# A planned attention, GLU and soft-MoE kernel: all short scores ahead of the pooling of v, the slots' input in two halves, two rules of the plan changed, and a new plan

## The chip, the cores and the metric

The kernel runs on one core of one Trainium2 chip. The metric is the device time of one execution in microseconds; of the kernel before, three runs are shown (median 522.01). A profile is one further execution, recorded by the hardware profiler. The core has a matrix engine (PE, with its weight loads PEld shown apart), three engines for elementwise work (DVE, ACT and POOL), a queue that issues all DMAs (SP), an on-chip memory for tiles, and eight banks of accumulation memory (`ps`), into which alone PE writes.

## The reference

```python
# attention: per (batch 4, head 8), 576 positions of 64
q_d, k_d, v_d = means over groups of 4 positions             # 144 positions: the "short" attention
out_up = repeat(softmax(q_d k_d^T / 8) v_d, 4)
out_local = softmax(q k^T / 8 where |i - j| < 4) v           # a band
x = (out_up + out_local)  as 2304 tokens x 512
# GLU: 512 -> 1536 -> 512
x = (x @ w_a * (x @ w_b)) @ w_out
# soft mixture of experts: 32 slots, 8 experts
logits = x @ phi
d = softmax(logits, over the tokens);  slot_input = d.T @ x  # 32 x 512
slot_out[e] = relu(slot_input[e] @ w1[e]) @ w2[e]            # 8 experts of 4 slots
out = softmax(logits, over the slots) @ slot_out
```

## The kernel before

The whole kernel is one program of small tasks. A task names its engine, an assumed duration, the tasks it depends on, a priority, and the buffers and banks that it takes and gives back. `Plan.run` plays the tasks through on assumed times and thereby fixes, once and for all, in which order each engine gets its instructions. `LOOK` says for each engine how much later than the earliest possible task another one may start and still win by priority; `WT` and `ALTW` say when a task may go to its second engine; `BATCH` says between which planned times, and how far, PE keeps the large products together instead of letting a small task in between; `PR_D`, `PR_P`, `SOON` and `CB` are priorities. On the chip each engine then takes its instructions strictly in that order and waits for what an instruction needs.

Where the plan sees PE idle early on, it puts in products without use (`warm`, L360, on the tile `acc`); they fill PE's queue up to about 42 us.

The work in the order of the tokens:

- **Short attention** (`plan_datt`), once per batch of 5 pairs. `plan_load` sums q and k over groups of four (L412 on DVE, or L415 and L417 on POOL) into `dT`. Then three groups n = 2, 0, 1 of `dscore` (L631), `dmax`, `dexp` (L662 on ACT), `drec`, `dnorm` (L320 on POOL, into `dk` and in place), `dptr` (transposes, L694, L698, L701), evictions into `dpt` and `dpr`, and `dout` (L735), which is evicted into `xd` (L750). In the first batch v is pooled by PE too: `dvmm` (L599, two tasks of 8 products each in the trace).
- **The band** (`plan_pair`), 20 pairs of 116 tokens: `score` (L449, L459), `smax` (L467), `ssub` (L473), `sexp` (L479), `ssum` (L483 to L487), `snorm` (L320), `ptr` (L497), `pev`, `pv` (L511), then the sum with `xd` (L520), split into a high and a low part, the tile `x`.
- **Weights** (`plan_piece`): 36 pieces of 512 KB arrive as 64-bit words in a ring of four staging buffers (SP, L861 and L863) and are rebuilt as floats by four instructions: `clow` (ACT, L834), `cabs` (ACT, L839), `cbits` (DVE, L843) and `csign` (DVE, L848), which gives the staging buffer back for the next load. Pieces 1 to 8 are the first third of w_a and w_b, 9 to 16 the second, 17 to 28 w_out transposed, 29 to 36 the last third. Pieces of w_a and w_b are then split into a high part (ACT) and a low part (POOL). Those of w_out are multiplied with phi (`omm`, L893, six tasks of two pieces) into `wpr` (L991, L996), so that the logits come from the GLU's product without w_out.
- **GLU** (`plan_unit`): 18 tiles x 3 thirds x 2 halves, 108 halves of 12 products each (L1023). Below, "0a" is a half with the first third of w_a, "2b" one with the last third of w_b, and a *run* is a number of halves that stand on PE with nothing between them. A half is followed by the product a*b (L1038), its transposes (L1045), an eviction (L315), and per two tiles by the logits (L1059) and a chain of softmax steps (`k1` to `k12`).
- **Tail** (`plan_tail`): the gathered sums are transposed (`atr`), the slots' input is 12 products 512 wide (`slot_in`, L1295), evicted (`si_ev`, L1302, ACT), transposed (`si_tr`, L1307), copied (`si_t`, L1313, DVE); then the experts' first layer (`l1`, L1328), the second (`l2`, L1417), and the output (L1464). Between these stand nine transposes of the gates (`ctr`, L1384), their high parts (`chi`, L1389, ACT) and their low parts (`clo`, L1396, DVE subtractions).

Of the kernel before, what the change touches and what calls it, by code (L numbers as in the profile page):

```python
# [22 lines left out]
NCH = NTILES // 2  # L23
# [252 lines left out]
def tile_attn_glu_softmoe(  # L276
# [30 lines left out]
    def psum(shape=(128, 512)):  # L307
        return pp.tile(list(shape), F32, tag="ps", name="ps")
# [261 lines left out]
    def plan_datt(b):  # L570
# [184 lines left out]
        vv = []  # L755
        for f in range(4):
            o = pr + 0.1 + 0.01 * f
            if b < WIDE:
                if f % 2:
                    continue  # L760
                tl = add("D", c_dma(524288), lambda f=f: dvload2(f // 2), prio=o - 2.0, acq=("g",), lat=2.0)
                tv = add("PE", 1.8, lambda f=f: dvmm(f), [tl], o, acq=("ps",), rel=("g",))
                vv.append(add(
                    "A", 0.37, lambda e, f=f: dvev(f, e), [tv, T.get(("dvp", b))], o, acq=() if f else ("dv",),
                    rel=("ps",), alt=("V", 0.4, WT["ev"]),
                ))
# [14 lines left out]
        for n in (2, 0, 1):  # L781
# [5 lines left out]
            tn.append(t1)  # L787
            t2 = add("V", 1.0 if n < 2 else 0.7, lambda n=n: dmax(n), [t1], o)
# [436 lines left out]
    def plan_tail():  # L1225
# [65 lines left out]
        def slot_in():  # L1291
            X["sps"] = ps = psum()
            for ft in range(12):
# [3 lines left out]
                    rhs=X.pop(("o", ft // 4, ft % 4)), start=(ft < 4), stop=(ft >= 8),  # L1297
                )

        def si_ev():  # L1300
            X["si"] = sb(mp, "a", (128, 512))
            nc.scalar.activation(out=X["si"], in_=X.pop("sps"), func=ACTF.Copy, scale=li)  # L1302

        def si_tr():
            X["stp"] = ps = psum((128, 4, 32))
            for dt in range(4):
# [8 lines left out]
        t = add("PE", 2.9, slot_in, ta + [t for n in range(3) for t in T["rows", n]], -2000, acq=("ps",))
        add("N", 0.0, lambda: [X.pop(("ot", n)) for n in range(3)], [t], 0, rel=("w8x",) * 3, lat=0.0)
        t = add("A", 0.58, si_ev, [t, t_sc], -50, acq=("a",), rel=("ps",))
        t = add("PE", 0.9, si_tr, [t], -2000, acq=("ps",), rel=("a",))
        t_si = add("V", 0.3, si_t, [t], -50, rel=("ps",))

        hs = []
        for eg in range(2):
            for hf in range(2):
# [50 lines left out]
        for i0 in range(0, NTILES, n):  # L1374
# [30 lines left out]
            tc_.append(add("V", 0.8, clo, [t], 50, rel=("ps",)))  # L1405
# [123 lines left out]
LOOK = dict(PE=0.07, V=0.23, A=0.03, G=0.79, D=0.1, N=0.0)  # L1529
WT = dict(pool=6.14, dvp=2.32, clo=4.65, clow=0.83, chi=7.15, norm=1.54, ev=0.86, xhi=7.17)  # L1530
# [12 lines left out]
CB = [-14.41, 0.63, -2.7, 0.8, 2.84, 13.81]  # L1543
# [50 lines left out]
```

## Time and profile before

| | us |
|---|---|
| median of 3 runs | 522.01 (521.02 to 522.11) |
| the profiled execution | 521.47 |
| its span in the trace | 519.7 |
| PE busy | 506.4 |
| DVE / ACT / POOL busy | 249.8 / 220.7 / 108.2 |

The span is what the trace covers; 1.77 us of the profiled execution lie around it. PE is busy nearly all the time, so the profile is to be read stage by stage: what PE's busy time consists of (early on, the products without use), where it waits, and what its tasks cost in the order in which they stand.

### The profile page before, as it was taken

Reading aid. Unit: us, or ns where it says so; the run is one execution under the profiler, and the core shown is the slowest. Engines: PE = TensorE matmul, PEld = TensorE weight load, DVE = VectorE, ACT = ScalarE, POOL = GpSimd, SP = SyncE. Lnnn points to the kernel's source line nnn. Section 1 sums busy time; section 2 is a strip of 40 time slices with the busy share of each in tenths; the row PEclk is TensorE's granted clock in tenths of the full one; section 3 lists DMA queues with packets and bytes.
Section 4 is the critical chain, followed back from the end, with each engine's and each line's share of the span. In section 5 each row is a group of like instructions: output and inputs, shape, how many; then the busy total and the mean of one; then the engine's idle time right before and its main releaser. Section 6 shows DMA issues by size and latency. Waiting matters only on the chain.

```text
span 519.7 us, 11193 instructions
## 1 busy us (share of the span) xinstructions
PE 506.4 (97%) x4605; PEld 387.7 (75%) x4605; DVE 249.8 (48%) x581; ACT 220.7 (42%) x533; POOL 108.2 (21%) x159
## 2 busy tenths in 40 slices
PE   8999998999999999999999999999999999989995
PEld 8888864677778777787777877878787778753484
DVE  5899888864387631453731341221234542245022
ACT  1888777864343432423532232222244532242132
POOL 0767657452133220330211000000000000020000
PEclk9999998999999999999999999999999999999997
DMA  8977688900152200321000000000076486999996
GB/s 318 389 224 259 215 262 283 325 34 0 42 180 90 77 2 1 108 81 55 26 2 0 21 21 2 21 1 1 1 279 205 145 343 255 370 399 420 420 356 252
DMA packets 23010, 84.25 MB, mean 162 GB/s; under 512 B 2992, under 2 KB 3888, under 8 KB 19376
## 3 DMA queue, kind: packets, MB, share of 16 engines
q1 hardware_dynamic: 22960, 83.54, 44.4%
q8 instruction: 36, 0.59, 0.5%
q14 instruction: 14, 0.11, 0.1%
HBM read 78.81 MB, written 4.72 MB: 161 GB/s over the span
## 4 chain that ended last, share of the span: by engine, by line
PE 87%; DMA 6%; DVE 2%; ACT 2%; issue 1%; POOL 1%; SPq 0%; ACTq 0%; DVEq 0%; POOLq 0%
PE ps L1023 55%; PE ps L1045 5%; PE ps L1059 3%; DMA w<-in_w_outt_dram 3%; DMA w<-in_moe_w_a_dram 3%; PE ps L1417 3%; PE ps L1328 3%; PE ps L511 3%; PE ps L360 2%; PE ps L1184 2%; PE ps L497 2%; PE ps L735 2%; PE ps L1464 1%; PE ps L459 1%; PE ps L631 1%; PE ps L694 1%
## 5 line engine op out<-in xcount | busy, mean ns | idle before, releaser
L1023 PE MATMUL ps<-w,x 128*128 128x512 f32 x1296 | 313.3, 396 | 0.4 <-ACT a L315 0.4
L1023 PEld LDWEIGHTS ps<-w,x 128*128 128x128 f32 x1296 | 239.3, 188 | 57.6 <-issue 5.4
L1038 DVE TENSOR_TENSOR g<-a,ps 128x512 f32<-128x512 f32 x51 | 34.8, 683 | 94.1 <-PE ps L1023 94.0
L315 ACT COPY a<-ps 128x512 f32<-128x512 f32 x51 | 29.8, 585 | 88.8 <-PE ps L1023 88.8
L315 ACT COPY gT<-ps 128x512 f32<-128x512 f32 x53 | 30.5, 586 | 49.3 <-PE ps L1045 49.2
L320 POOL TENSOR_TENSOR e<-e,mx 128x512 f32<-128x512 f32 x20 | 20.9, 1044 | 90.5 <-DVE mx L487 78.3
L320 POOL TENSOR_TENSOR w<-cv,w 128x512 fp32r<-128x512 f32 x24 | 31.1, 1303 | 23.8 <-ACT w L315 20.0
L1172 POOL TENSOR_TENSOR cn<-ce,cs 128x64 f32<-128x64 f32 x9 | 2.6, 293 | 145.3 <-DVE cs L1169 100.5
L1045 PE MATMUL ps<-cst,g 128*128 128x128 f32 x216 | 32.3, 277 | 0.0
L834 ACT ACTIVATE w<-w 128x512 uint32<-128x512 uint32 x36 | 24.5, 684 | 15.4 <-DMA w<-in_w_outt_dram 6.6
L1045 PEld LDWEIGHTS ps<-cst,g 128*128 128x128 f32 x216 | 24.9, 141 | 7.3 <-issue 1.6
L843 DVE SCALAR_TENSOR_TENSOR ps<-ps,w 128x512 uint32<-128x512 uint32 x36 | 24.9, 692 | 5.3 <-ACT ps L839 5.0
L848 DVE SCALAR_TENSOR_TENSOR cv<-w,ps 128x512 uint32<-128x512 uint32 x36 | 24.7, 687 | 2.8
L360 PE MATMUL ps<-acc 128*128 128x128 f32 x150 | 21.7, 297 | 1.2 <-POOL acc L355 1.2
L839 ACT ACTIVATE ps<-w 128x512 f32<-128x512 f32 x36 | 22.9, 640 | 0.0
L360 PEld LDWEIGHTS ps<-acc 128*128 128x128 f32 x150 | 19.9, 208 | 1.9 <-POOL acc L355 1.2
L320 DVE TENSOR_TENSOR x<-xn,x 128x256 fp32r<-128x256 f32 (+16 forms) x36 | 17.4, 512 | 4.8 <-ACT x L315 4.4
L412 DVE TENSOR_REDUCE dT<-qk 128x116 f32<-128x464 f32 (+1 forms) x28 | 16.3, 623 | 5.6 <-DMA qk<-in_qk_dram 5.6
L467 DVE TENSOR_REDUCE mx<-ps 128x4 f32<-128x256 f32 x40 | 15.0, 417 | 7.5 <-PE ps L459 7.4
L843 DVE SCALAR_TENSOR_TENSOR ps<-ps,w8x 128x512 uint32<-128x512 uint32 x12 | 8.4, 696 | 20.2 <-ACT ps L839 20.2
L520 DVE TENSOR_TENSOR xn<-ps,xd 128x232 f32<-128x232 f32 (+1 forms) x40 | 13.9, 392 | 8.5 <-PE ps L511 8.4
L1059 PE MATMUL ps<-gT,wpr 128*32 128x256 f32 x216 | 17.2, 390 | 0.8 <-ACT gT L315 0.8
(156 smaller groups left out, 586.9 us busy)
## 6 DMA issues: line engine op xcount, KB each, us to landing
w<-in_moe_w_dram SPq DMA_DIRECT2D x15, 1024.0 KB, 8.5
w8x<-in_moe_w_dram SPq DMA_DIRECT2D x13, 1024.0 KB, 8.7
qk<-in_qk_dram SPq DMA_DIRECT2D x18, 480.0 KB, 5.1
w<-in_moe_w_a_dram SPq DMA_DIRECT2D x12, 512.0 KB, 5.1
w<-in_moe_w_b_dram SPq DMA_DIRECT2D x12, 512.0 KB, 4.7
w<-in_w_outt_dram SPq DMA_DIRECT2D x12, 512.0 KB, 5.0
w8x<-in_moe_w_out_dram SPq DMA_DIRECT2D x12, 512.0 KB, 4.8
bv<-in_vw_dram SPq DMA_DIRECT2D x20, 256.0 KB, 3.6
```

Source lines behind the costliest of these rows:

```text
L315: nc.scalar.copy(out=out, in_=in_)
L320: (nc.vector if e == "V" else nc.gpsimd).tensor_tensor(**a)
L360: nc.tensor.matmul(out=X["warm"][:, 0:128], lhsT=acc[:, 0:128], rhs=acc[:, 0:128], start=True, stop=True)
L412: nc.vector.tensor_reduce(out=dst, in_=view(src, dims, off), op=ALU.add, axis=AX.X)
L834: nc.scalar.activation(out=d, in_=d, func=ACTF.Copy, scale=31 / 32 * 2.0 ** -29, bias=-0.26)
L839: nc.scalar.activation(out=f, in_=words(raw)[0].bitcast(F32), func=ACTF.Abs, scale=2.0 ** -112)
L843: nc.vector.scalar_tensor_tensor(out=d, in0=d, scalar=3, in1=words(raw)[1], op0=ALU.logical_shift_left, op1=ALU.bitwise_or)
L848: nc.vector.scalar_tensor_tensor(out=out.bitcast(U32), in0=words(raw)[0], scalar=0x80000000, in1=f.bitcast(U32), op0=ALU.bitwise_and, op1= ...
L1023: nc.tensor.matmul(out=ps, lhsT=X[x, i][:, hq, :], rhs=X["w", fc, ab, wi][:, hq, :], start=(hq == 0 and m == 0), stop=(hq == 3 and m == 2),)
L1038: nc.vector.tensor_tensor(out=X["g", c, fc][:, t, :], in0=X.pop(("a", i, fc)), in1=X.pop(("mm", i, fc, 1)), op=ALU.mult)
L1045: nc.tensor.transpose(out=ps[:, fi, :], in_=X["g", c, fc][:, t, fi * 128:fi * 128 + 128], identity=ident)
L1059: nc.tensor.matmul(out=X["lg", c][fi * 32:fi * 32 + 32, :], lhsT=wpr[:, fc * 4 + fi, :], rhs=gT[:, fi, :], start=(fc == 0), stop=(fc == 2),)
```

## The change

Five edits.

1. In the first batch the two poolings of v by PE get one more dependence: the score task n = 1, which is the last of the three. So all scores of the short attention come ahead of them.
2. `slot_in` becomes two tasks, columns 0 to 255 and 256 to 511, 12 products each; eviction, transposes and copy are halved with it, and the first layer's steps 0 and 1 depend on the first half alone, 2 and 3 on the second.
3. The low parts of the gates' transposes wait: the first four for the last update of `acc`, the others for the copy of the second half of the slots' input.
4. `slot_in` and the halves declare themselves as products on 32 columns (`part`), and some assumed durations change.
5. The plan's numbers are new (`LOOK`, `WT`, `BATCH`, `SOON`, `PR_D`, `PR_P`, `CB`), and with them nearly every engine's order.

```diff
+            if n == 1:
+
+                for tv in vm:
+                    tv["deps"].append(t1)
...
-        def slot_in():
-            X["sps"] = ps = psum()
+
+        def slot_in(h):
+            X["sps", h] = ps = psum((128, 256))
             for ft in range(12):
                 j = ft % 4
                 nc.tensor.matmul(
                     out=ps[j * 32:j * 32 + 32, :], lhsT=X["aT"][:, ft % 3, (ft // 3) * 32:(ft // 3) * 32 + 32],
-                    rhs=X.pop(("o", ft // 4, ft % 4)), start=(ft < 4), stop=(ft >= 8),
+                    rhs=X["o", ft // 4, ft % 4][:, h * 256:h * 256 + 256], start=(ft < 4), stop=(ft >= 8),
                 )
...
+        for h in range(2):
+            t = add(
+                "PE", 1.4, lambda h=h: slot_in(h), ta + [t for n in range(3) for t in T["rows", n]] + tsl, -2000,
+                acq=("ps",), part="128x32",
+            )
+            tsl.append(t)
+            t = add("A", 0.37, lambda h=h: si_ev(h), [t, t_sc], -50, acq=() if h else ("a",), rel=("ps",))
+            t = add("PE", 0.45, lambda h=h: si_tr(h), [t], -2000, acq=("ps",), rel=("a",) if h else ())
+            t_si.append(add("V", 0.2, lambda h=h: si_t(h), [t], -50, rel=("ps",)))
...
-                        "PE", 0.94, lambda dt=dt, l1=l1: l1(dt), [t_si, w, t], 3000 + eg * 2 + hf,
+                        "PE", 0.94, lambda dt=dt, l1=l1: l1(dt), [t_si[dt // 2], w, t], 3000 + eg * 2 + hf,
...
-            tc_.append(add("V", 0.8, clo, [t], 50, rel=("ps",)))
+
+            tc_.append(add("V", 0.86, clo, [t, T["k12", NCH - 1] if i0 < 8 else t_si[1]], 50, rel=("ps",)))
...
-LOOK = dict(PE=0.07, V=0.23, A=0.03, G=0.79, D=0.1, N=0.0)
+LOOK = dict(PE=0.03, V=0.15, A=0.02, G=0.31, D=0.1, N=0.0)
...
-BATCH = [0.81, 5.46, 104.04, 490.05]
+BATCH = [1.79, 5.53, 134.98, 463.93]
...
-PR_D = [-98.14, 21.53, 74.67, 96.59]
+PR_D = [-98.14, 44.26, 78.1, 98.72]
```

PE's queue at the start, from the first short scores (`dT`) on; a row with a minus stands in the kernel before alone, one with a plus in the changed one. L360 are products without use, `g` is v, `w_218` and `w_228` hold the short attention's exponentials, and `e` the band's.

```order
 L631 MATMUL ps<-dT_94,dT_91 32x144 x8
+L360 MATMUL ps<-acc 128x128 x4
+L631 MATMUL ps<-dT_94,dT_91 128x144 x4
+L360 MATMUL ps<-acc 128x128 x4
+L631 MATMUL ps<-dT_94,dT_91 128x144 x4
+L360 MATMUL ps<-acc 128x128 x7
 L599 MATMUL ps<-g,cst 128x256 x4
-L631 MATMUL ps<-dT_94,dT_91 128x144 x4
+L694 MATMUL ps<-cst,w_228 128x128 x2
+L701 MATMUL ps<-cst,dk 128x16
 L599 MATMUL ps<-g,cst 128x256 x4
-L360 MATMUL ps<-acc 128x128 x5
```

The three groups of scores now stand together ahead of both poolings (L599); the last of them stood behind both, and behind the first transposes. Over the whole program PE has 71 instead of 75 products without use in this order (each is two instructions in the trace).

ACT's queue at the start, before and then after (`w_82` and `w_83` are staging buffers; after, L839 is `clow` and L844 `cabs`).

```order
L662 ACTIVATE w_218,dm<-ps,dn 128x144 x2
L479 ACTIVATE e<-e 128x512
L315 COPY dv<-ps 128x256
L834 ACTIVATE w_82<-w_82 128x512
L839 ACTIVATE ps<-w_82 128x512
L662 ACTIVATE w_218,dm<-ps,dn 128x144 x4
L315 COPY dv<-ps 128x256
```

```order
L839 ACTIVATE w_82<-w_82 128x512
L844 ACTIVATE ps<-w_82 128x512
L479 ACTIVATE e<-e 128x512
L662 ACTIVATE w_228,dm<-ps,dn 128x144 x10
L839 ACTIVATE w_82<-w_82 128x512
L479 ACTIVATE e<-e 128x512
L315 COPY dv<-ps 128x256
```

The first weight piece has moved ahead of all exponentials, and all ten exponentials of the short attention (2 + 4 + 4) stand in one block. On SP the load of that piece has moved ahead of the loads of v.

PE's queue in the tail, before and then after. `gT` holds the transposed sums and then the slots' input, `a` the evicted slots' input or the gates, `acc` the sums.

```order
L1272 MATMUL ps<-cst,acc 128x128 x3
L1384 MATMUL ps<-cst,a 128x128 x4
L1295 MATMUL ps<-w8x,gT 32x512 x12
L1384 MATMUL ps<-cst,a 128x128 x6
L1307 MATMUL ps<-cst,a 128x32 x4
L1328 MATMUL ps<-w8x,gT 32x512 x12
```

```order
L1277 MATMUL ps<-cst,acc 128x128 x3
L1400 MATMUL ps<-cst,a 128x128 x4
L1301 MATMUL ps<-w8x,gT 32x256 x12
L1400 MATMUL ps<-cst,a 128x128 x2
L1301 MATMUL ps<-w8x,gT 32x256 x12
L1316 MATMUL ps<-cst,a 128x32 x2
L1400 MATMUL ps<-cst,a 128x128 x2
L1316 MATMUL ps<-cst,a 128x32 x2
L1344 MATMUL ps<-w8x,gT 32x512 x4
L1400 MATMUL ps<-cst,a 128x128 x2
L1344 MATMUL ps<-w8x,gT 32x512 x8
```

The six products with the gates that stood together behind `slot_in` now stand singly between the halves' steps, and the first layer (L1344) begins before the last of them.

## Rows read from the trace of the kernel before

**Rows 1.** The page, busy time of each engine (share of the span, instructions).

```profile
PE 506.4 (97%) x4605; PEld 387.7 (75%) x4605; DVE 249.8 (48%) x581; ACT 220.7 (42%) x533; POOL 108.2 (21%) x159
```

**Rows 2.** Windows: length, busy time per engine (instructions), granted clock, DMA share, GB/s.

```profile
46.47:98.89 52.42, 49.84 (x358) 35.68 (x354) 44.73 (x83) 39.97 (x76) 31.45 (x46) 0.97 0.81 271
115.96:461.21 345.25, 343.98 (x2813) 269.84 (x2811) 135.51 (x338) 119.38 (x313) 40.00 (x64) 1.00 0.27 95
```

**Rows 3.** Timeline of the start: start, duration, engine, line [idle before, releaser].

```profile
15.64 0.68 ACT L834 ACTIVATE w<-w 128x512 uint32<-128x512 uint32 x1 [1.43 <-DMA w<-in_moe_w_a_dram]
...
17.60 0.69 DVE L848 SCALAR_TENSOR_TENSOR cv<-w,ps 128x512 uint32<-128x512 uint32 x1
...
19.80 1.28 PE L360 MATMUL ps<-acc 128*128 128x128 f32 x10
...
20.72 0.43 ACT L662 ACTIVATE w<-ps,dn 128x144 f32<-128x144 f32 x1
...
22.06 0.27 ACT L662 ACTIVATION_READ_ACCUMULATOR w<-ps,dn 128x1 f32 x1
...
23.48 1.04 POOL L320 TENSOR_TENSOR w<-w,dm 128x512 f32<-128x512 f32 x1
...
30.20 0.41 ACT L750 ACTIVATE xd<-ps 128x288 f32<-128x288 f32 x1 [0.62 <-PE ps L735]
...
31.17 1.28 PE L511 MATMUL ps<-pt,bv 64*64 64x58 f32 x64
...
35.24 3.01 PE L1023 MATMUL ps<-w,x 128*128 128x512 f32 x12
...
46.47 5.75 PE L1023 MATMUL ps<-w,x 128*128 128x512 f32 x24
```

**Rows 4.** Timeline, 82 to 95 us: PE's wait, piece 28, the last `omm`.

```profile
82.69 0.63 PE L497 MATMUL ps<-cst,e 128*128 128x128 f32 x4 [2.21 <-ACT wpr L996]
...
90.79 0.69 DVE L848 SCALAR_TENSOR_TENSOR cv<-w,ps 128x512 uint32<-128x512 uint32 x1
...
94.58 1.05 PE L893 MATMUL ps<-cv,phis 128*32 128x512 f32 x4
```

**Rows 5.** Windows, the 4 us behind that wait (columns as in rows 2).

```profile
84.00:88.00 4.00, 4.00 (x14) 2.56 (x11) 2.69 (x5) 3.17 (x6) 3.61 (x9) 0.63 0.87 332
```

**Rows 6.** Timeline, 108 to 119 us: piece 36, its low part, the first 2b.

```profile
108.48 0.69 DVE L848 SCALAR_TENSOR_TENSOR cv<-w,ps 128x512 uint32<-128x512 uint32 x1
...
109.09 1.14 DVE L412 TENSOR_REDUCE dT<-qk 128x112 f32<-128x448 f32 x2
...
112.27 2.54 POOL L320 TENSOR_TENSOR w<-cv,w 128x512 fp32r<-128x512 f32 x2 [0.37 <-ACT w L315]
112.57 0.63 ACT L315 CAST w<-cv 128x512 fp32r<-128x512 f32 x1
...
115.96 3.01 PE L1023 MATMUL ps<-w,x 128*128 128x512 f32 x12
```

**Rows 7.** Timeline of PE: a run of one half and one of three, with followers.

```profile
99.70 2.98 PE L1023 MATMUL ps<-w,x 128*128 128x512 f32 x12
102.61 0.64 PE L1059 MATMUL ps<-gT,wpr 128*32 128x256 f32 x8
...
330.88 8.45 PE L1023 MATMUL ps<-w,x 128*128 128x512 f32 x36
339.26 0.64 PE L1059 MATMUL ps<-gT,wpr 128*32 128x256 f32 x8
```

**Rows 8.** Timeline of the tail: `slot_in` to the first layer, and `l2`.

```profile
467.92 2.78 PE L1295 MATMUL ps<-w8x,gT 128*32 128x512 f32 x24
...
471.38 0.69 ACT L1302 ACTIVATE a<-ps,li 128x512 f32<-128x512 f32 x1
...
473.62 2.78 PE L1328 MATMUL ps<-w8x,gT 128*32 128x512 f32 x24 [0.42 <-DVE gT L1313]
...
492.00 1.91 PE L1417 MATMUL ps<-g,gT 128*32 128x256 f32 x32
```

More of the change, by code (lines that the diff above doesn't have):

```diff
@@ L753, in doev @@
             )
-        vv = []
+        vv, vm = [], []
         for f in range(4):
@@ L762, in plan_datt @@
                 tv = add("PE", 1.8, lambda f=f: dvmm(f), [tl], o, acq=("ps",), rel=("g",))
+                vm.append(tv)
                 vv.append(add(
@@ L1296, in slot_in, with si_ev @@
                     out=ps[j * 32:j * 32 + 32, :], lhsT=X["aT"][:, ft % 3, (ft // 3) * 32:(ft // 3) * 32 + 32],
-                    rhs=X.pop(("o", ft // 4, ft % 4)), start=(ft < 4), stop=(ft >= 8),
+                    rhs=X["o", ft // 4, ft % 4][:, h * 256:h * 256 + 256], start=(ft < 4), stop=(ft >= 8),
                 )
[L1300 to L1306, printed above, removed]
+        def si_ev(h):
+            if h == 0:
+                X["si"] = sb(mp, "a", (128, 512))
+            nc.scalar.activation(
+                out=X["si"][:, h * 256:h * 256 + 256], in_=X.pop(("sps", h)), func=ACTF.Copy, scale=li
+            )
@@ L1307, in si_tr @@
+        def si_tr(h):
+            X["stp", h] = ps = psum((128, 2, 32))
+            for dt in range(2 * h, 2 * h + 2):
                 nc.tensor.matmul(
-                    out=ps[:, dt, :], lhsT=X["si"][:, dt * 128:dt * 128 + 128], rhs=rep32, start=True, stop=True
+                    out=ps[:, dt % 2, :], lhsT=X["si"][:, dt * 128:dt * 128 + 128], rhs=rep32, start=True, stop=True
                 )
-            X.pop("si")
-        def si_t():
-            nc.vector.tensor_copy(out=X["siT"], in_=X.pop("stp"))
@@ L1315, in plan_tail, with si_t @@
[L1315 to L1319, printed above, removed]
+            if h == 1:
+                X.pop("si")
+        def si_t(h):
+            nc.vector.tensor_copy(out=X["siT"][:, 2 * h:2 * h + 2], in_=X.pop(("stp", h)))
@@ new lines, in plan_tail @@
+        tsl, t_si = [], []
+        for h in range(2):
+            t = add(
+                "PE", 1.4, lambda h=h: slot_in(h), ta + [t for n in range(3) for t in T["rows", n]] + tsl, -2000,
+                acq=("ps",), part="128x32",
+            )
+            tsl.append(t)
+            t = add("A", 0.37, lambda h=h: si_ev(h), [t, t_sc], -50, acq=() if h else ("a",), rel=("ps",))
+            t = add("PE", 0.45, lambda h=h: si_tr(h), [t], -2000, acq=("ps",), rel=("a",) if h else ())
+            t_si.append(add("V", 0.2, lambda h=h: si_t(h), [t], -50, rel=("ps",)))
@@ L1321, in plan_tail @@
+        add("N", 0.0, lambda: [X.pop(("ot", n)) for n in range(3)], tsl, 0, rel=("w8x",) * 3, lat=0.0)
         hs = []
@@ L1528 @@
 LATE = 2
-LOOK = dict(PE=0.07, V=0.23, A=0.03, G=0.79, D=0.1, N=0.0)
-WT = dict(pool=6.14, dvp=2.32, clo=4.65, clow=0.83, chi=7.15, norm=1.54, ev=0.86, xhi=7.17)
+LOOK = dict(PE=0.03, V=0.15, A=0.02, G=0.31, D=0.1, N=0.0)
+WT = dict(pool=6.34, dvp=3.04, clo=6.09, clow=2.69, chi=8.31, norm=1.55, ev=2.84, xhi=6.88)
 ALTW = dict(V=99.0, A=0.0, G=1.0)
@@ L1533 @@
 WIDE = 1
-BATCH = [0.81, 5.46, 104.04, 490.05]
+BATCH = [1.79, 5.53, 134.98, 463.93]
 OQ = 2
-SOON = [-98.94, -98.94]
-PR_D = [-98.14, 21.53, 74.67, 96.59]
-PR_P = (-16.57, 4.24)
+SOON = [-99.09, -98.94]
+PR_D = [-98.14, 44.26, 78.1, 98.72]
+PR_P = (-18.44, 4.3)
 CORD = [(0, ab, m) for ab in range(2) for m in range(4)] + [(1, ab, m) for ab in range(2) for m in range(4)]
@@ L1542 @@
 CORD += [(2, ab, m) for ab in range(2) for m in range(4)]
-CB = [-14.41, 0.63, -2.7, 0.8, 2.84, 13.81]
+CB = [-14.09, 0.63, -2.41, 0.8, 2.65, 7.95]
 def cpr(c):
```

## The prediction

> **What bounds the kernel now.** I read the page first: PE is busy 97% of the span [rows 1], so the time is the sum of what stands in PE's queue, plus its waits, and the question at each stage is whether PE or something else is late. Cut into stages, the windows say the following. From 115.96 to 461.21 us PE is busy 343.98 of 345.25 us [rows 2]: in two thirds of the kernel nothing is ever late for PE, and only the length of its own queue counts there. From 46.47 to 98.89 it is busy 49.84 of 52.42 us, at a mean granted clock of 0.97 [rows 2]: here the ring of weight pieces feeds it, and it has lost time. Up to 46.47 us PE looks busy, but part of that is products without use, such as the ten at 19.80 us, 0.128 us each [rows 3]; the start is bound by the chain that makes the first token tile. The timeline of the start shows this chain: the last group of exponentials begins at 20.72, its normalisation on POOL ends at 24.52 (23.48 + 1.04), the second eviction of the short attention ends at 30.61 (30.20 + 0.41), the first product with v is at 31.17, the first GLU half at 35.24, and the first pair of 0b halves at 46.47 [rows 3]. The last window that matters is the tail, a chain again: from `slot_in` at 467.92 to the first layer at 473.62 [rows 8].
>
> **The start, edits 1 and 5.** Before, the last group of scores stands behind both poolings of v, and its exponentials behind a weight piece, for whose data ACT waited 1.43 us until 15.64 [rows 3]. After, the three groups stand together, and ten exponentials run in one block. The last group took 1.61 us for four, from 20.72 to 22.33 (22.06 + 0.27) [rows 3]; groups 0 and 1, eight of the ten, begin at about 15, when DVE has their maxima, and end near 18. That is 4 us earlier, but it doesn't reach PE whole. POOL's queue is next: the sums of v's rest, three normalisations of the short attention and two of the band, back to back, 23.5 instead of 24.52 at the end. Then DVE: the maxima and subtractions of two more pairs now stand ahead of the last small eviction, which ends near 25.9, so the first `dout` is at 26.0, the second eviction ends near 30.2 and the product with v starts near 30.3 instead of 31.17 [rows 3]. PE's own queue would allow about the same: four products without use fewer, two instructions each, 8 x 0.128 = 1.0 us [rows 3]. From there to the first 0b pair the queue holds the same tasks and the same twelve pairs of products without use as before, so I take -0.9 us at 46.47, with bounds -1.9 (both gains in full) and +0.8 (each piece of w_a now waits behind the softmax on DVE; see the slower rival).
>
> **The ring, 46 to 116 us, edit 5.** Before, PE lost 2.21 us in one wait at 82.69 [rows 4], 0.37 in a second, and the 4 us that followed ran at 0.63 [rows 5]: 0.37 of 4.00 = 1.48 us. Together 4.06. The order after has the same tasks and the same number of runs of halves up to the first 2b (16, two of them double). Without a wait the last `omm` would come at 94.58 [rows 4] - 0.9 - 4.06 = 89.6. It needs piece 28, which was ready at 91.48 (90.79 + 0.69) [rows 4]. The ring has four buffers and sends a load when a piece is done, so I let it keep its pace and take the same 91.5: PE waits 1.9 there and the gain is 3.1. The changed order has the last two `omm` next to each other, and 0.65 us of band scores behind instead of ahead of them, which takes that from the gain: -2.4 at the first 2b. This half has a floor of its own: piece 36 was done at 109.17 (108.48 + 0.69), then a cast of 0.63 and the two low parts that take 2.54 on POOL [rows 6] give 112.3; 115.96 - 2.4 = 113.6 is above it. So at this place -2.4 us, the start included; bounds -3.6 (the floor) and +3.4 (below).
>
> **The middle, edit 5.** From the first 2b to the last logits, nothing waits on PE [rows 2], so the order itself sets the time. A run of one half takes 102.61 - 99.70 = 2.91 us to its follower, one of three 339.26 - 330.88 = 8.38 with the same follower [rows 7]. A half more in a run costs (8.38 - 2.91) / 2 = 2.735, so each new run costs 0.175 on top. By the two orders this stretch has 22, 11, 10 and 4 runs of one, two, three and four halves before, and 11, 6, 17 and 4 after: 47 runs for 90 halves become 38. Nine times 0.175 is -1.6 us. The small tasks are the same in number. What could eat it is a small task that comes later behind a longer run and whose chain is then late; the elementwise engines are busy for 135.51, 119.38 and 40.00 of 345.25 us here [rows 2], which hides a shift of 3 to 6 us. Bounds 0 and -2.5 (0.28 a run, if a boundary also costs the small tasks 0.1).
>
> **The tail, edits 2 to 4.** Before, 467.92 to 473.62: `slot_in` 2.78, eviction done at 472.07 (471.38 + 0.69), then transposes and a copy, 1.55 to the first layer; 5.70 us in a chain, with the gates' products in its gaps [rows 8]. After, the first half's products end at 469.3 (half of 2.78), its eviction beside the second half's products; these and two gates' products (0.2) end at 470.9. Then the first half's transposes (0.5, of the 1.55 a third), gates (0.2), the second half's transposes (0.5), and the first layer's step 0 begins near 472.1, once the copy of the first half, long done, and PE's queue allow. Its four products last 0.93 (2.78 for three steps [rows 8]), gates 0.2, so step 1 begins at 473.2; before it did at 473.62 + 0.93 = 474.55. The gain is 1.35, and I write 1.4 us. The half evictions are not in the trace; they lie between 0.35 (half of 0.69) and 0.69 [rows 8], I take 0.4, and either value is hidden by 1.57 us of PE work for the first half. The held-back subtractions cost nothing: they free DVE for the copies, and their results are used by the output, behind both layers. DVE still has eight of them between the sums and the copies; the first copy can start near 471.4, and I count on them being done by then, as all before it were (the copy of before followed its transposes at once). What releases weights for the second layer moves by +0.2, against a use that lies 20 us later. Bounds: -2.0 and 0.
>
> Two halves load the same 32-column weights twice. The trace has 32 products 256 wide in 1.91 us, 0.06 each, with their loads [rows 8]; 24 of 512 took 2.78, 0.116 each, so a half as wide costs half and the 24 loads more are hidden. The Trainium skill ("TensorE: Matmul & The Clock Gate", section on LDWEIGHTS) puts a load at its columns over 1.2 GHz whatever the rows, which speaks against the split: as an estimate 24 loads of 32 columns would be 0.64 us if they were exposed, and the tail's gain 0.8 instead of 1.4. The rows say hidden, and I go by them.
>
> **Sum.** -2.4 - 1.6 - 1.4 = -5.4 us against the profiled execution's 521.47 (519.7 and 1.77 around it) gives 516.1. The median shown is 0.54 higher; by it the time is 516.6.
>
> **Rivals.**
> The ring eats the start. The first piece is done near 21.8 instead of 18.29 (17.60 + 0.69) [rows 3], as DVE now does the softmax first; DVE has room to catch up by piece 5, but if it stays 2 to 3 us behind, every `omm` waits and the first 2b comes at the same time as before. Then only -1.6 - 1.4 remain: 519.0. For it: the wait of before came from this ring. Against: POOL loses six sums, and pieces 5 and on depend on the loads as before.
> The ring runs ahead. If the pieces follow PE's earlier start by 1 us and `omm` doesn't wait, 2b is at its floor: -3.6 - 1.6 - 1.4 = -6.6, 515.4.
> The plan's gain isn't there: new waits in the middle cancel the saved runs, the start gains nothing, and the change is its tail: 520.6.
> Slower: the ring falls behind for good. By the order six of the sums of q and k go from POOL to DVE, 0.57 each (1.14 for two) [rows 6], 3.4 us; with the 3.5 us of the first piece the last one is done at 109.17 + 6.9 = 116.1 and 2b at 119.3 instead of 115.96. This 3.3 cancels the middle and the tail, and if PE then waits as at 82.69 and its clock falls as in rows 5, another 1.5 is lost: 522.0 + 0.3 + 1.5 = 523.8. It decides from 2b at 119.0 on. Against it: by the order only three of these sums stand ahead of the last piece on DVE.
>
> **How the numbers follow.** The forecast has 0.48, the ring that eats the start 0.24, the ring ahead 0.15, the tail alone 0.06, slower 0.07. Its own range is 515.4 to 518. Within 0.2% (1.04 us, what a measurement of this kernel can tell from no change) falls part of the tail alone and of the slower case. Faster 0.87, same 0.06, slower 0.07. The range 514.0 to 520.4 leaves out the slower case and the ends of the others.
>
> **What would show it.** After: no idle of 2.2 us on PE near 80, perhaps one of 1 to 2 before the last `omm` near 90; the first 0b pair near 45.6; the first 2b near 113.6 (116 or later if the ring ate it, 112.4 if it ran ahead); from there to the last logits 1.6 us less than 345.25, still without waits; from `atr` to step 1 of the first layer 1.4 us less. A granted clock below 1 behind a wait, a wait of PE for a weight load in the first or second layer, or idle in the middle would make it wrong.

## The result, and the profile after

The changed kernel took 517.85 us, median of 5 runs (517.0 to 518.86), against 522.11 for the kernel before beside it: a ratio of 0.9912, 95% interval 0.9889 to 0.9934. That is 4.3 us less; forecast were 5.4, and the time lies in the range and in the likeliest case's own range. In a second series (e5 below) it was 518.98 against 521.95, ratio 0.9935 (0.9915 to 0.9954): 3.0 us less. The two intervals overlap, so the series alone do not show two different gains; the two profiles differ, and the traces show in which stage. The profiled execution of e1 (527.09 us) was a slow one, and no mean below takes it in.

The profiled execution took 517.0 us with a span of 515.3. The page, busy time of each engine, to be held against [rows 1]:

```profile
PE 501.0 (97%) x4621; PEld 386.5 (75%) x4621; DVE 247.8 (48%) x587; ACT 223.7 (43%) x538; POOL 98.7 (19%) x138
```

PE is busy 5.4 us less than before, but the span is only 4.4 shorter: PE waits 1.0 us more than it did. The stages say where. First the start. The timeline of PE shows first the band product of before, which waits for ACT's cast of the constants, and then, of after, the same product, the first product with v and the first pair of 0b halves.

```profile
7.16 0.30 PE L449 MATMUL ps<-band,eyeb 64*64 64x256 bf16 x4 [0.54 <-ACT band L373]
```

```profile
7.68 0.30 PE L449 MATMUL ps<-band,eyeb 64*64 64x256 bf16 x4 [1.17 <-ACT band L373]
...
30.65 1.28 PE L511 MATMUL ps<-pt,bv 64*64 64x58 f32 x64
...
46.04 5.72 PE L1028 MATMUL ps<-w,x 128*128 128x512 f32 x24
```

The pair comes 0.43 us earlier than the 46.47 of [rows 3]. But the profile of after started 0.52 late, since its constants landed later. From the first band product it takes 46.04 - 7.68 = 38.36 us, before 46.47 - 7.16 = 39.31: 0.95 less. The windows of this stage, before and then after (columns as in [rows 2]), tell what became shorter:

```profile
7.16:46.47 39.31, 38.95 (x598) 34.08 (x597) 36.08 (x86) 30.55 (x75) 22.50 (x26) 1.00 0.88 307
```

```profile
7.68:46.04 38.36, 38.01 (x590) 32.77 (x590) 35.54 (x89) 30.32 (x73) 22.66 (x28) 1.00 0.89 313
```

PE is idle for 0.36 us of it before and 0.35 after. All of the gain, 0.94, is work that PE no longer has, and the eight instructions that it has less are the four products without use (8 x 0.128 = 1.0 by [rows 3]).

Then the ring. The timeline of ACT and PE from 66 to 114 us:

```profile
66.52 3.04 PE L1028 MATMUL ps<-w,x 128*128 128x512 f32 x12
...
70.06 0.62 ACT L844 ACTIVATE ps<-w 128x512 f32<-128x512 f32 x1
72.09 0.67 ACT L839 ACTIVATE w<-w 128x512 uint32<-128x512 uint32 x1 [1.41 <-DMA w<-in_w_outt_dram]
72.67 0.56 ACT L315 COPY a<-ps 128x512 f32<-128x512 f32 x1
...
73.28 3.02 PE L1028 MATMUL ps<-w,x 128*128 128x512 f32 x12 [1.86 <-ACT a L315]
...
90.10 2.10 PE L898 MATMUL ps<-cv,phis 128*32 128x512 f32 x8
...
92.76 0.67 PE L459 MATMUL ps<-qk 64*58 64x64 f32 x32 [0.32 <-DMA qk<-in_qk_dram]
...
113.67 3.02 PE L1028 MATMUL ps<-w,x 128*128 128x512 f32 x12
```

The wait of 2.21 at 82.69 [rows 4] is gone, but PE now waits 1.86 at 73.28. What it waits for is an eviction (L315) whose half PE had finished at 69.6. ACT was free at 70.7, but takes its queue in order and stood 1.41 us at a `clow` whose load had not landed. The Trainium skill ("TensorE: Matmul & The Clock Gate", section on the architectural detail, queue depths) calls ACT's and DVE's queues strict FIFO; these rows agree. The first 2b stands at 113.67, 2.29 us earlier than in [rows 6]. The windows from the first pair of 0b to the first 2b, before and then after:

```profile
46.47:115.96 69.49, 66.91 (x477) 48.11 (x473) 57.58 (x108) 53.17 (x103) 42.04 (x56) 0.98 0.70 232
```

```profile
46.04:113.67 67.63, 65.22 (x476) 47.40 (x474) 60.14 (x110) 53.70 (x101) 32.91 (x34) 1.00 0.71 236
```

PE's idle time is 2.58 us before and 2.41 after: the waits have moved rather than gone. What the stage gained, 1.86 us, is 1.69 of busy time, and 1.48 of that is the half clock of [rows 5], which after does not have.

The middle, first 2b to last logits, in one window (columns as in [rows 2]):

```profile
113.67:457.84 344.17, 341.69 (x2810) 270.65 (x2810) 130.74 (x337) 121.60 (x320) 40.52 (x66) 1.00 0.27 96
```

It is 1.08 us shorter than the 345.25 of [rows 2]; PE's busy time in it fell by 2.29. The difference is a wait that before did not have. (For the slots' input w_out is loaded once more here, row by row, and rebuilt like a piece.) The timeline of the wait:

```profile
423.49 3.00 PE L1028 MATMUL ps<-w,x 128*128 128x512 f32 x12
...
425.10 0.65 ACT L839 ACTIVATE w8x<-w8x 128x512 uint32<-128x512 uint32 x1 [2.12 <-DMA w8x<-in_moe_w_out_dram]
...
426.80 0.70 DVE L848 SCALAR_TENSOR_TENSOR ps<-ps,w8x 128x512 uint32<-128x512 uint32 x1 [2.29 <-ACT ps L844]
427.41 0.68 DVE L1043 TENSOR_TENSOR g<-a,ps 128x512 f32<-128x512 f32 x1
...
428.14 0.66 PE L1050 MATMUL ps<-cst,g 128*128 128x128 f32 x4 [1.21 <-DVE g L1043]
```

PE waits 1.21 us for a product a*b, whose half was done at 426.5, but which on DVE stands behind the conversion of a row of w_out; DVE waits for ACT, and ACT stood 2.12 us at a load. A late load here holds up work that has nothing to do with it, through two in-order queues.

The tail, PE's timeline from the last logits to step 1 of the first layer:

```profile
457.84 0.70 PE L1109 MATMUL ps<-lgs,cst 128*128 128x256 f32 x2 [0.49 <-ACT lgs L1105]
...
463.37 0.55 PE L1277 MATMUL ps<-cst,acc 128*128 128x128 f32 x3 [0.23 <-DVE acc L1199]
...
464.48 1.50 PE L1301 MATMUL ps<-w8x,gT 128*32 128x256 f32 x24
465.91 0.44 PE L1400 MATMUL ps<-cst,a 128*128 128x128 f32 x2
466.28 1.50 PE L1301 MATMUL ps<-w8x,gT 128*32 128x256 f32 x24
...
468.94 1.06 PE L1344 MATMUL ps<-w8x,gT 128*32 128x512 f32 x8
...
470.31 1.92 PE L1344 MATMUL ps<-w8x,gT 128*32 128x512 f32 x16
```

Step 1 begins 12.47 us behind the last logits; before it was 474.51 (its record in the trace) - 461.21 = 13.30. Of the 0.83 less, 0.77 lie between `atr`, at 463.37 here, and step 1: 6.94 us against 474.51 - 466.80 = 7.71, by the `atr` of before:

```profile
466.80 0.55 PE L1272 MATMUL ps<-cst,acc 128*128 128x128 f32 x3 [0.30 <-DVE acc L1194]
```

The rest, to the end of the span, is 44.99 against 45.19. The sum of the stages is -2.29 - 1.08 - 0.83 - 0.20 = -4.4, the difference of the spans.

### The profile page after: what moved, and what is told of

It reads as the page before. It is cut to its first block, busy times and chain, and to the rows that moved or that the text cites. A ratio compares the mean times of both kernels' runs of the same rounds, so it can differ in the third digit from the quotient of the medians.

```text
span 515.3 us, 11223 instructions
## 1 busy us (share of the span) xinstructions
PE 501.0 (97%) x4621; PEld 386.5 (75%) x4621; DVE 247.8 (48%) x587; ACT 223.7 (43%) x538; POOL 98.7 (19%) x138
## 4 chain that ended last, share of the span: by engine, by line
PE 81%; DVE 7%; DMA 6%; ACT 3%; issue 2%; POOL 0%; SPq 0%; DVEq 0%; ACTq 0%; POOLq 0%
PE ps L1028 48%; PE ps L1050 4%; PE ps L1434 3%; PE ps L1344 3%; PE ps L1064 3%; PE ps L360 3%; DMA w8x<-in_moe_w_out_dram 2%; PE ps L511 2%; PE ps L1189 2%; DVE ps L848 2%; PE ps L735 2%; PE ps L497 2%; PE ps L459 2%; PE ps L631 1%; PE ps L1481 1%
## 5 line engine op out<-in xcount | busy, mean ns | idle before, releaser
L1028 PE MATMUL ps<-w,x 128*128 128x512 f32 x1296 | 309.9, 395 | 1.9 <-ACT a L315 1.9
L315 ACT COPY a<-ps 128x512 f32<-128x512 f32 x51 | 29.9, 586 | 108.6 <-PE ps L1028 108.5
L315 ACT COPY gT<-ps 128x512 f32<-128x512 f32 x54 | 31.1, 584 | 34.4 <-PE ps L1050 34.0
L839 ACT ACTIVATE w<-w 128x512 uint32<-128x512 uint32 x36 | 24.7, 685 | 15.4 <-DMA w<-in_w_outt_dram 6.7
L412 DVE TENSOR_REDUCE dT<-qk 128x116 f32<-128x464 f32 (+1 forms) x34 | 19.9, 623 | 6.1 <-DMA qk<-in_qk_dram 6.1
L844 ACT ACTIVATE ps<-w 128x512 f32<-128x512 f32 x36 | 22.8, 633 | 0.0
L360 PE MATMUL ps<-acc 128*128 128x128 f32 x142 | 21.4, 300 | 1.2 <-POOL acc L355 1.2
L360 PEld LDWEIGHTS ps<-acc 128*128 128x128 f32 x142 | 18.8, 207 | 2.6 <-POOL acc L355 1.2
L520 DVE TENSOR_TENSOR xn<-ps,xd 128x232 f32<-128x232 f32 (+1 forms) x40 | 13.9, 391 | 13.2 <-PE ps L511 13.2
L839 ACT ACTIVATE w8x<-w8x 128x512 uint32<-128x512 uint32 x12 | 8.1, 679 | 20.8 <-DMA w8x<-in_moe_w_out_dram 20.7
```

Source lines behind the costliest of these rows:

```text
L315: nc.scalar.copy(out=out, in_=in_)
L360: nc.tensor.matmul(out=X["warm"][:, 0:128], lhsT=acc[:, 0:128], rhs=acc[:, 0:128], start=True, stop=True)
L412: nc.vector.tensor_reduce(out=dst, in_=view(src, dims, off), op=ALU.add, axis=AX.X)
L839: nc.scalar.activation(out=d, in_=d, func=ACTF.Copy, scale=31 / 32 * 2.0 ** -29, bias=-0.26)
L844: nc.scalar.activation(out=f, in_=words(raw)[0].bitcast(F32), func=ACTF.Abs, scale=2.0 ** -112)
L1028: nc.tensor.matmul(out=ps, lhsT=X[x, i][:, hq, :], rhs=X["w", fc, ab, wi][:, hq, :], start=(hq == 0 and m == 0), stop=(hq == 3 and m == 2),)
```

## The experiments

Twelve series ran, eleven of other kernels and one of after again, each beside runs of before and not all on the same chip; so a time is compared by its ratio, or with another of the same series. The intervals of the ratios reach 0.14 to 0.3% to either side, so each experiment is read first by its own stage in its profile, which is one execution. The marks, all taken from PE's records in the profiled executions: from the first band product to the first pair of 0b; from there to the first 2b; from there to the last logits; from there to step 1 of the first layer.

| kernel | 0b pair | first 2b | last logits | step 1 | median, ratio to before |
|---|---|---|---|---|---|
| before | 39.31 | 69.49 | 345.25 | 13.3 | |
| after | 38.36 | 67.63 | 344.17 | 12.5 | 517.85, 0.9912 |
| e1 numbers only | 38.62 | 74.05 | 346.41 | 13.7 | 521.2, 0.9964 |
| e2 slot_in whole | 38.44 | 68.78 | 346.41 | 13.2 | 520.51, 0.9948 |
| e3 not held | 38.76 | 68.81 | 346.88 | 12.9 | 519.84, 0.9937 |
| e4 before, BATCH | 39.45 | 69.37 | 343.44 | 13.7 | 520.0, 0.9936 |
| e5 after again | 38.50 | 69.39 | 344.19 | 12.5 | 518.98, 0.9935 |
| e6 rows late | 38.63 | 68.75 | 343.36 | 12.4 | 518.35, 0.9939 |
| e7 before, filled | 39.52 | 69.09 | 345.25 | 13.3 | 522.1, 1.0008 |
| e8 start + 1 us | 38.90 | 71.67 | 344.13 | 12.5 | 519.57, 0.9960 |
| e9 before, filled less | 39.20 | 68.30 | 345.23 | 13.3 | 522.12, 0.9989 |
| e10 fewer idle products | 37.20 | 70.62 | 346.79 | 12.5 | 520.87, 0.9970 |
| e11 both | 37.96 | 72.67 | 343.35 | 12.4 | 518.55, 0.9922 |
| e12 after, old BATCH | 38.26 | 67.85 | 346.17 | 12.4 | 519.88, 0.9957 |

**e1: the plan's numbers alone.** The code of before with edit 5.

```diff
-BATCH = [0.81, 5.46, 104.04, 490.05]
+BATCH = [1.79, 5.53, 134.98, 463.93]
... (LOOK, WT, SOON, PR_D, PR_P, CB likewise)
```

> The code of before with the plan numbers of after alone (edit 5 without edits 1 to 4). The order then has 38 runs of halves behind the first 2b instead of 47, as after has. The forecast's terms: middle -1.1 to -1.6, ring without the wait of 2.21 and the half clock -1.5 to -2.4, tail 0: 518.2 to 519.5 us. Rival: the numbers only fit the changed code (two edits move what stands around the first batch), the ring of before stays: under -1.3 us, 520.8 or more.

Measured: ratio 0.9964 (0.9942 to 0.9985), 1.3 us by the medians. The instructions stand in the same order as in after on every engine up to the tail, although edit 1 is missing: with the new numbers the scores already come ahead of the poolings, and the new dependence moves nothing. All that is gained ahead of the tail belongs to edit 5. The time itself missed the forecast of 518.2 to 519.5 and is the rival's (520.8 or more), but not for the rival's reason, as the order is that of after. By the ratios e1 is 1.5 to 2.7 us behind the two series of after, of which the tail explains 1.2 (13.7 against 12.5); the rest is within the intervals. In the profiled execution PE waited 3.06 us at 97.81 for a load of q and k, and the clock of 100 to 104 was 0.72.

**e2 and e3: the tail's two edits apart.** e2 has `slot_in` and what follows it whole again (edits 2 and 4 undone); e3 has

```diff
-            tc_.append(add("V", 0.86, clo, [t, T["k12", NCH - 1] if i0 < 8 else t_si[1]], 50, rel=("ps",)))
+            tc_.append(add("V", 0.8, clo, [t], 50, rel=("ps",)))
```

> After with slot_in, its eviction, transposes and copy whole again (edits 2 and 4 undone); by the order nothing ahead of the tail changes. The forecast's tail term of 1.4, of which 0.9 shows between the last logits and step 1 of the first layer in the two traces: +0.9 to +1.4 us on after, 518.7 to 519.3, all of it between atr and step 1. Rival: the 24 loads more of 32 columns and the small pieces eat what the halves save, and the 0.9 came from the held-back subtractions: within 0.3 us of after, 517.6 to 518.1.

> After with the subtractions not held back (edit 3 undone); the order differs only on DVE and POOL in the tail: twelve subtractions instead of eight between the sums and the first copy of the slots' input. At 0.44 us each the first copy would come 1.8 us later on DVE than the eight let it, of which 1.2 us was idle before it: +0.4 to +0.7 us, 518.3 to 518.6, as a wait of PE at step 0 of the first layer. The forecast as written (the holding back costs nothing and gains nothing by itself): within 0.3 us of after.

Measured: 0.9948 (0.9928 to 0.9968) and 0.9937 (0.9916 to 0.9958), against 0.9935 and 0.9912 for after. The intervals overlap; the tails are clear. From the last logits to step 1: 13.3 before, 13.2 with the holding back but without the halves (e2), 12.9 with the halves but without the holding back (e3), 12.5 with both. So the halves bring 0.7, less than the 0.9 to 1.4 expected of them, and the rival is refuted. In e2 PE's timeline is that of [rows 8] again:

```profile
467.90 2.78 PE L1301 MATMUL ps<-w8x,gT 128*32 128x512 f32 x24
...
473.57 2.78 PE L1335 MATMUL ps<-w8x,gT 128*32 128x512 f32 x24 [0.38 <-DVE gT L1319]
```

In e3 the loss has the expected size, 0.43, but the expected place was wrong. The twelve subtractions ended just in time for the first copy (step 0 came 5.57 us behind `atr`, as in after); the loss stands ahead of `atr`, where two subtractions on DVE delay the last sum:

```profile
465.55 0.86 DVE L1412 TENSOR_TENSOR g<-ps,g 32x256 fp32r<-32x256 f32 x2
...
466.84 0.61 DVE L1199 SCALAR_TENSOR_TENSOR acc<-acc,al,ps 128x384 f32<-128x384 f32 x1
```

```profile
467.51 0.55 PE L1277 MATMUL ps<-cst,acc 128*128 128x128 f32 x3 [0.66 <-DVE acc L1199]
```

From the last logits to `atr` it is 5.95 us here, against 5.53 in after, but 5.59 in before. The holding back thus repairs what the new numbers of edit 5 would have cost at this place; against before it gains next to nothing.

Both profiles also show the wait near 428 us longer than in after, 1.88 in e2 and 2.31 in e3, and the clock fell behind it: over the 30 us from 420 on it was 0.94 in both, and PE's busy time in the middle is 1.6 us above that of after. The wait and the window of e3:

```profile
430.26 0.66 PE L1050 MATMUL ps<-cst,g 128*128 128x128 f32 x4 [2.31 <-DVE g L1043]
```

```profile
420.00:450.00 30.00, 27.69 (x128) 21.99 (x128) 8.73 (x15) 10.09 (x21) 0.00 (x0) 0.94 0.78 291
```

**e4 and e12: the four BATCH numbers alone**, put into before (e4), and those of before put back into after (e12).

> Before with the four BATCH numbers of after and nothing else: 37 runs of halves behind the first 2b instead of 47, the order ahead of it unchanged. The forecast's 0.175 us a run: -1.75 us, 520.3. The two traces, in which PE was busy 2.29 us less there for nine runs less (0.25 a run): -2.5 us, 519.6. Rival: longer runs make a small task late and PE waits as long as it saved: -0.5 to +0.5 us, 521.6 to 522.6.

> The counterpart of e4: after with the four BATCH numbers of before, all else as in after; the order then has 50 runs of halves behind the first 2b instead of 38. PE's own queue from the first 2b to the last logits, waits taken off, should grow by 12 times 0.18 to 0.25 (e4 gave 0.22 a run, the two first traces 0.25): from 342.9 or 343.0 us in the profiles of after to 345.1 to 346.0. Whether the gate product near 428 us still waits is open: without that wait the time is 1.0 to 1.8 us over after, with it 2.2 to 3.0 over.

Measured: 0.9936 (0.9912 to 0.9959) and 0.9957 (0.9943 to 0.9972). The window of the middle, e4 and then e12:

```profile
116.21:459.65 343.44, 341.73 (x2813) 270.24 (x2811) 134.11 (x337) 120.11 (x314) 39.73 (x64) 1.00 0.28 96
```

```profile
113.76:459.93 346.17, 344.88 (x2811) 269.46 (x2811) 134.28 (x338) 121.18 (x319) 40.42 (x66) 1.00 0.27 95
```

Where the clock stays at 1.00, PE's busy time there goes by the number of runs: 341.73 with 37, 341.69 with 38 (after), 343.98 with 47 (before), 344.88 with 50. That is 0.23 to 0.27 us a run. From after to e12 the busy time grew by 3.19 us for twelve runs, a little more than expected; e12 has no wait near 428, so of these 3.2 us after loses 1.21 again in that wait. By the medians BATCH alone takes 2.5 us off before, and its ratio, 0.9936, cannot be told from that of the whole change (0.9912 and 0.9935). The stage itself is 1.8 shorter; the profile of e4 lost 1.6 us in the tail, behind a clock of 0.75 from 470 to 475 us, whose cause was not found.

**e5: after again**, as reference for the next three.

> After unchanged, on the chip and beside the runs of the next three, as their reference: 517.0 to 519.0 us. Its profiled execution is expected to show again one wait of PE for a gate product near 428 us, of 1.2 us or longer (in the profiles of e1, e2 and e3, which have the same order there, it took 1.82, 1.88 and 2.31, and the granted clock of 420 to 450 us was 0.94).

Measured as expected, 1.24 at 430.41. But the ring stage took 69.39 us in this profile, as much as before: PE was idle for 3.54 us of it, against 2.41 in the first profile, most of it in three places:

```profile
74.01 3.01 PE L1028 MATMUL ps<-w,x 128*128 128x512 f32 x12 [1.32 <-ACT a L315]
```

```profile
92.89 1.04 PE L898 MATMUL ps<-cv,phis 128*32 128x512 f32 x2 [0.91 <-DVE cv L853]
```

```profile
95.03 0.67 PE L459 MATMUL ps<-qk 64*58 64x64 f32 x32 [0.86 <-DMA qk<-in_qk_dram]
```

**e6: the wait near 428.** One number: how late the plan takes the rows of w_out to land.

```diff
-            ts_ = add("D", c_dma(524288), stage, [T["ost"]], prio=2000 + n, acq=("ost",), lat=2.0)
+            ts_ = add("D", c_dma(524288), stage, [T["ost"]], prio=2000 + n, acq=("ost",), lat=4.0)
```

> After with one number changed: the plan takes the loads of w_out's rows to land 4.0 us behind their issue instead of 2.0, as the trace shows them (4.3). Up to the first layer PE's order is the same; only ACT and DVE have the conversions of these rows later between their other work. Theory: the wait near 428 comes from ACT, which stands at a conversion whose load has not landed, with the gates' copies queued behind; then the wait goes, -1.2 us where it was short and -3 to -4 where the clock fell behind it: 514 to 516.5. Rival: the conversions only move into later gaps and make a gate product there late, or the rows are late for slot_in: within 0.5 us of after.

Measured: 518.35, ratio 0.9939 (0.9915 to 0.9963). The mechanism holds: the product a*b now starts on DVE as soon as PE has finished its half, ahead of the conversion, and the wait is 0.44.

```profile
427.93 0.69 DVE L1043 TENSOR_TENSOR g<-a,ps 128x512 f32<-128x512 f32 x1 [1.91 <-PE ps L1028]
428.53 0.69 DVE L848 SCALAR_TENSOR_TENSOR ps<-ps,w8x 128x512 uint32<-128x512 uint32 x1
...
428.76 0.63 PE L1050 MATMUL ps<-cst,g 128*128 128x128 f32 x4 [0.44 <-DVE g L1043]
```

The middle is 0.83 us shorter than in e5, at the same PE busy time. In the medians it is 0.6, within what the series can tell from nothing, and the forecast of 514 to 516.5 was missed; the 3 to 4 us hoped for in executions with a fallen clock did not show.

**e7 and e9: the half clock behind 82.69 in before.** Products without use in the place of the wait, five and three of them.

```diff
+            nc.tensor.matmul(out=X["wp", 1][64:128, 0:384], lhsT=acc[:, 0:64], rhs=acc, start=True, stop=True)
```

> Before with five products without use (384 columns each, about 2 us) in the place of the wait of 2.21 us at 82.69, nothing else moved. The granted clock behind it should then stay at 1.0 and PE be 1.5 us earlier at 88. Forecast (PE's lost time at half clock is part of the gain of 4.06): the first 2b 1.5 us earlier, near 114.5, 520.6 us. Rival: the half run at 96.01 waits for ACT, which waits for a load of the ring, so what PE gains at 88 it waits at 96: first 2b within 0.3 us of before, 521.8 to 522.4.

> As e7, with three products without use instead of five: by the 3.44 us that five took in e7, three take 2.06, which is no more than the wait of 2.21 at 82.69 in before. In e7 the transposes behind the wait began 1.09 us later after the omm ahead of it than in before, the granted clock stayed at 1.0, and from that omm to the first 2b it took 36.06 us instead of 36.53. Theory (what the half clock takes is on the path): from the third omm to the first 2b 34.9 to 35.2 us, and 1.3 to 1.6 us off before's time. Rival (PE waits for the ring's load later instead): 36.2 to 36.5 us, the time within 0.4 us of before.

Five took 3.44 us instead of 2, longer than the wait: 0.34 a record, as the 0.128 of [rows 3] for a third of the columns could have told. Three fitted. PE's timeline in e9:

```profile
79.63 1.05 PE L893 MATMUL ps<-cv,phis 128*32 128x512 f32 x4
80.61 2.15 PE L360 MATMUL ps<-acc 128*64 128x384 f32 x6
82.95 0.63 PE L497 MATMUL ps<-cst,e 128*128 128x128 f32 x4 [0.20 <-ACT wpr L996]
...
89.88 0.63 PE L1045 MATMUL ps<-cst,g 128*128 128x128 f32 x4 [0.53 <-DVE cv L848]
...
115.18 3.01 PE L1023 MATMUL ps<-w,x 128*128 128x512 f32 x12
```

The clock of 84 to 88 us was 1.00 in both, 0.63 in [rows 5]. From the `omm` at 79.63 to the first 2b it is 35.55 us, before, from the same `omm` at 79.43, 36.53: of the 1.48 us that the half clock took, about 1.0 reaches the first 2b, and 0.53 comes back as a wait for a piece of the ring. Each theory gets a part. The medians show neither (1.0008 and 0.9989, interval of the second 0.9969 to 1.001).

**e8: one microsecond more in the start.** Four products without use more at 41.5 us.

> After with four more products without use (8 x 0.128 = 1.0 us) on PE ahead of the second half run, at 41.5 us. It prices the start: if what the start gains or loses reaches the first 2b, as the forecast has it, the first pair of 0b, the first 2b and the end come 1.0 us later. Rival: the wait near 73 us takes it up (1.86 us in the profile of after), and the first 2b and the end stay within 0.3 us.

Not settled. The first pair of 0b came 38.90 us behind the band product, 0.4 later than the mean of this order, and the median is 0.6 over e5 with overlapping intervals (0.9941 to 0.998 here). The profile had the wait near 75 us at 2.09, the half behind it took 4.61 us instead of 3.02, and PE waited 2.45 more at 98.21 for a load of q and k; that covers what was to be measured.

```profile
75.36 4.61 PE L1028 MATMUL ps<-w,x 128*128 128x512 f32 x12 [2.09 <-ACT a L315]
```

**e10 and e11: a better version?** Fewer products without use, alone and with e6.

```diff
-WARM = [1.0, 60.0, 0.23, 6.5]
+WARM = [1.0, 60.0, 0.3, 6.5]
```

> After with the plan counting 0.30 us for a product without use instead of 0.23: 52 of them in the first 46 us instead of 71, nothing else moved. In after's trace several stand on PE's queue while what follows them is ready (ten records of 1.31 us ahead of the first product with v, whose operands were there from 24.6 us and its buffer from 29.9). Theory: the first pair of 0b comes 0.5 to 1.5 us sooner behind the first band product (38.4 to 38.7 in the runs of this order). Of that, by e8, about half reaches the end: -0.3 to -0.8 us. Rival: PE then waits for the same chain as long as it idled, or the granted clock falls in the gaps: 0, or up to 2 us slower.

> e10 and e6 together: fewer products without use at the start, and the loads of w_out's rows planned to land at 4.0 us. Expected the sum of both, -0.5 to -1.5 us on after, with the wait near 428 us at 0.4 instead of 1.2 to 2.3 and the granted clock of 420 to 450 us at 1.00; on before -3.5 to -5.5 us. Rival: the start's gain ends at the waits for the ring near 74 and 93 us, and only e6's 0.4 to 0.8 remain.

e10 missed: the start is 1.3 us shorter as expected, but the time is 520.87, ratio 0.9970 (0.9941 to 1.0): 1.8 to 3.0 us behind the two series of after, at or beyond the end of its rival's range. Its profile, the longest of its runs, shows PE waiting 2.14 us at the first band product, and behind it a clock that after did not lose:

```profile
10.00:20.00 10.00, 10.00 (x81) 8.77 (x80) 9.55 (x29) 6.17 (x24) 3.51 (x7) 0.84 1.05 400
```

That stretch is part of the start, though, which is shorter all the same. What makes this profile 8.7 us longer than that of after stands further on: 3.0 in the ring, 2.6 in the middle (the wait near 428, 2.17 here, with a clock of 0.94 over 420 to 450 us), and 3.5 behind step 1, where the clock of 515 to 524 us was 0.50 and the last sixteen large products of the output took 3.68 us, in after 2.00:

```profile
515.40 3.68 PE L1481 MATMUL ps<-ht,g 128*128 128x128 f32 x16 [0.69 <-DVE ht L1462]
```

Whether fewer products without use have a part in these, or whether they are the spread of one execution, is open.

e11 came to 518.55, ratio 0.9922 (0.9894 to 0.995), 3.9 us less than before, as expected, but not to be told from after; the wait near 428 and the fallen clock there are gone as expected. So no version here beats after beyond doubt.

## Why the prediction was right, and where it was not

The verdict and the size were right. The start and the ring have the right size, but not by the way described; the middle is two errors that partly cancel; the tail works as described and was put too large.

**Start, -0.9.** Right in size. From the first band product to the first pair of 0b the six profiles with after's order there (after, e2, e3, e5, e6, e12) have 38.26 to 38.76, mean 38.49; the four with before's order 39.20 to 39.52, mean 39.37: -0.88. The chain came much as described: the last exponentials ended at 18.50 and the second eviction at 29.86 us (forecast were 18 and 30.2), in a profile that started 0.52 late. But it is not what PE stood at. In both orders PE's own queue fills this stage, products without use included, and the gain is the four of these that went, which the prediction had only as a second limit (1.0 us). That both calculations gave about the same is why the number holds. Whether the old chain would have allowed PE four products fewer, no run here shows. And edit 1, to which the term was put down beside edit 5, has no part in it: e1 has the same order without it. What the prediction could have seen is that a dependence may be fulfilled already by the priorities that come with it.

**Ring, -2.4 at the first 2b with the start.** The first profile has -2.29; in that the agreement is partly luck, as this profile is the fastest of its order. Counted from the band product, six profiles of this order have a mean of -1.8 (107.03 against 108.80), between -0.9 and -2.8. The sum also holds a slip: the second wait, 0.37 at 96.01, lies behind the last `omm` at 94.58 and cannot bring that `omm` forward; without it the wait there would be 1.5 instead of 1.9 and the term -2.8. And the way was another. The prediction took the 4.06 us of waits and half clock as all recoverable but for one wait before the last `omm`. That wait was 0 to 1.0 long; a wait of 1.3 to 1.9 stands at 73 to 74 instead, and not for a piece itself, but for an eviction behind a piece's `clow` in ACT's queue. PE idles in this stage about as long as before or longer (2.4 to 3.5 us in the six profiles, 2.6 before), and what is gained is the half clock. The ring itself kept its pace, as assumed: piece 28 was ready at 91.11, before at 91.48. The rival "the ring eats the start" has its result in e5, whose first 2b, at 115.91, stands where before's did, but not its cause: the late first piece (22.34 in after, 22.86 in e5) was made up by the fifth (35.46 and 35.99; before 35.71), and e5 lost its time further on (piece 14 at 64.71, in after at 63.24).

**Middle, -1.6.** Two steps failed, the price of a run and "nothing waits". Nine runs fewer saved 2.29 us of PE's time, 0.25 each, near the upper bound of 0.28 and not the 0.175 taken. The rows of [rows 7] price only the way from a half to its follower; what else a boundary costs, no view here shows by itself. Against it stands the new wait of 1.21 near 428, of the kind named there ("a small task that comes later behind a longer run") though by another way: the small task was ready, and DVE stood at a conversion. The 1.08 that is left is within the bounds because the two errors partly cancel; by the prediction's own list of signs, idle time in the middle speaks against its account. In e2, e3 and e10 this wait was 1.88 to 2.31, with a clock of 0.94 over the 30 us around it, and the middle was then 1.2 to 1.6 us longer than before. That it can turn the term's sign was not in the bounds (0 and -2.5).

**Tail, -1.4.** Measured -0.83, and -0.77 from `atr` to step 1, the stretch that the prediction names. The chain came as described, but most of its pieces a little longer: from `slot_in` to step 1 it takes 470.31 - 464.48 = 5.83 us and not the 5.3 of the prediction. The two pairs of gates' products that stand there alone took 0.37 each instead of 0.2, which is 0.34 of the miss; the rest is spread over the products of the halves, the transposes and step 0. A half `slot_in` takes 1.43 us to its follower (464.48 to 465.91), two of them 2.86, which is 0.15 more than the whole one of before (467.92 to 470.63). The Trainium skill ("TensorE: Matmul & The Clock Gate", section on LDWEIGHTS) gives, as an estimate, 0.64 us for the 24 loads more if they were exposed; at most 0.15 of it shows, so they are nearly hidden, as the rows said, not wholly. "The held-back subtractions cost nothing" is right against before: they repair 0.4 us that the new numbers would cost ahead of `atr` (e3), and the gain is that of the halves.

**Sum.** -5.4 forecast, -4.4 by the spans: 0.5 too much in the middle, 0.6 in the tail, 0.1 in the ring, and 0.2 gained behind step 1 that was not counted.

## What to carry to other kernels

When an engine takes its queue strictly in order, look at what stands in front of the instruction that everyone waits for: here a conversion whose load was late delayed an eviction that could have started 2 us earlier, and the profile then names the eviction. Where a stage became shorter, ask first whether idle time or busy time went; a chain that was made shorter need not be what the engine stood at. Price a reordering by the busy time of a whole stage in several orders, not by one pair of rows; here four orders gave a clean cost per boundary. And when runs of one kernel differ by as much as the change is worth, find the stage that varies and compare the others without it.

## What was not expected of the hardware

Behind a wait of about 2 us the clock may or may not fall, and its length alone does not tell: behind 2.09 at 75 us in e8 the next half took 4.61 (granted clock 0.63 over its first 4 us, so mostly the lower level of 1.2 GHz), behind 2.11 at the same place in e11 it took its usual 3.01 (clock 1.00).

```profile
75.18 3.01 PE L1028 MATMUL ps<-w,x 128*128 128x512 f32 x12 [2.11 <-ACT a L315]
```

Behind 2.45 (e8, at 98.21) the clock stayed at 1.00, behind 1.89 (e11, at 110.44) it was 0.63 over the next 4 us. Why, no run here settles; it makes a wait of this size a risk of some 1.5 us more (1.48 behind 82.69 in before, 4.61 - 3.01 = 1.60 here).
